# Attention followed by a feed-forward block on one core: outputs turned by the DMA, 288-token units, a smaller mask build

## The chip, the core and the metric

The kernel runs on one core of one Trainium2 chip. The metric is device time in microseconds of one launch. The program has five engines with queues of their own: TensorE (PE in the profile; PEld is its weight loading), VectorE (DVE), ScalarE (ACT), GpSimd (POOL) and SyncE (SP). POOL issues the loads and SP the stores; both sets of transfers run on the core's 16 DMA engines.

## What is computed

Eight batches of eight-head attention over 576 tokens with 64 features per head, and then a linear chain of matrix products over all 4608 tokens:

```python
batch, n_heads, seq, head_dim = (8, 8, 576, 64)
scores = scale * np.matmul(q, k.transpose(0, 1, 3, 2))
mask_plain = (rel >= 0) & (rel < 32)                                  # heads 0 to 3
mask_dil = (rel >= 0) & (rel < 32 * 4) & (rel % 4 == 0)               # heads 4 to 7
attn = softmax(np.where(masks, scores, -1e9))
x = np.matmul(attn, v).transpose(0, 2, 1, 3).reshape(B * S, H * D)    # 4608 x 512
a, b = x @ w1, x @ w2                                                 # 512 x 1024 each
out = (a * b @ w3) @ w_out                                            # 1024x1024, 1024x512
```

A query sees 32 keys. In a dilated head those keys lie four tokens apart, so a head splits into four residue classes of 144 tokens, each of them a plain sliding window.

## The kernel before, in words

All matrix data is bf16, sums are f32. The two last products are merged once: wf = w3 @ w_out (the W3 tasks, L494 to L516), so the feed-forward block is two products up (A with w1, B with w2), an elementwise product, and one product down with wf.

**Attention.** A batch has four steps: plain heads (u=0) and dilated heads (u=1), each in two halves of 288 tokens (hf), a half being three query blocks of 96. DVE turns q, k (and v of batches 0 and 1) to feature-major form with 32x32 transposes (`turn`, L276 and L289). Each step then is: scores on PE (`scores`, 24 small matmuls, L344), exponentials on ACT (`exps`, L354), mask product on DVE (`masks`, L360; batches 0 and 1 add a bias on PE before, L327, and skip it), values on PE (`values`, L377, two groups of six), reciprocal and normalization on DVE (L395, L401) into the tile `xo` (tokens by features), transposition back on PE (`back`, six matmuls with the identity, L412) into a PSUM bank, and a copy of that bank into the tile XT (features by tokens): `keep`, two copies of 288 columns per step, on ACT (L429) or DVE (L431). v of batches 2 to 7 comes straight from HBM into `vp` by many short runs (L196, L210).

**Feed-forward.** It works in tiles of 512 tokens (TB), nine of them. For each of eight feature blocks f it makes A (four matmuls of 512 columns, L442), copies it to SBUF on ACT (`copy_a`, L453, tile asb), makes B (four more), and multiplies both on DVE (`gate`, L457) into gt. Four `down` products per tile (eight matmuls of 512 columns, L464) give 128 output rows each; ACT copies them out (L475, osb) and SP stores them (L486). XT holds the tokens of all chunks in residue order (all tokens with remainder 0 by 4, then 1, 2, 3), so `store` scatters rows back with a step of four. Plain heads are brought into that order too: their queries are read with a strided pattern inside `scores`, and their mask has a pattern of its own for each half.

**Order.** All work is put into tasks, and `Plan.run` makes one static order for every engine from written-out durations, latencies and priorities (`add`). All PE results but the scores go through four PSUM banks ("places"): a task with slot=True takes a bank, which is free again when all tasks that read it are over. Scores have four banks of their own. Batches 2 and later are paced: a step's scores may start only after a certain A product (LEAD). POOL issues, in this order: q and k of batch 0 for u=0, the identity, q and k for u=1, v, the masks (`build_masks`, L241 to L263), w1/w2, w_out, w3, and then the loads of batch 1 and later.

Of the kernel before, what the change touches and what calls it, by code (L numbers as in the profile page):

```python
# [26 lines left out]
TB = 512  # L27
BIG = 30000.0
BIASED = 2
LEAD = 2.25  # L30
# [13 lines left out]
class Plan:  # L44
# [13 lines left out]
    def run(self):  # L58
# [22 lines left out]
        while len(order) < n:  # L81
            progress = True
            while progress:
                progress = False
                for e in engines:
# [25 lines left out]
                    for u in users[id(t)]:  # L111
                        left[id(u)] -= 1
                        if not left[id(u)]:
                            r = max(d.end + d.lat for d in u.deps)
                            waiting[u.eng].append((r, u))
# [12 lines left out]
def kernel(  # L128
# [19 lines left out]
    NT = n_tok // TB  # L148
# [16 lines left out]
    XT = const.tile([P, DCH, n_tok], BF16, name="XT")  # L165
    ident = const.tile([P, P], BF16, name="ident")
    mask = const.tile([P, 3, 3, QB], BF16, name="mask")
    vps = [const.tile([P, H, 6, PITCH], BF16, name=f"vp{i}") for i in range(2)]
    bias = const.tile([P, 3, 3, QB], BF16, name="bias")
# [4 lines left out]
    warm = const.tile([P, TB], BF16, name="warm")  # L174
# [65 lines left out]
    def build_masks():  # L240
        nc.gpsimd.memset(mask, 1.0)  # L241
        for i in range(3):
            m = mask[:, i, :, :]
            if i < 2:
                m, pat = m.rearrange("p m (r t) -> p m r t", r=4), [[0, 3], [1, 4], [4, 24]]
            else:
                pat = [[0, 3], [1, QB]]
            nc.gpsimd.affine_select(
                out=m, in_=m, compare_op=AL.is_ge, fill=0.0,
                base=32, pattern=pat, channel_multiplier=-1,  # L250
            )
            nc.gpsimd.affine_select(
                out=m, in_=m, compare_op=AL.is_ge, fill=0.0,
                base=-1, pattern=[[-a, n] for a, n in pat], channel_multiplier=1,
            )
            if i != 1:
                nc.gpsimd.memset(mask[0:32, i, 0, :], 0.0)
        late = mask[:, 2, 1, QB // 2 : QB]
        nc.gpsimd.affine_select(
            out=late, in_=late, compare_op=AL.is_ge, fill=0.0,  # L260
            base=-(32 + QB // 2), pattern=[[0, QB // 2]], channel_multiplier=1,
        )
        nc.gpsimd.tensor_scalar(  # L263
            out=bias, in0=mask, scalar1=-1.0, scalar2=BIG, op0=AL.add, op1=AL.mult
        )
# [47 lines left out]
    class Step:  # L313
# [4 lines left out]
        def kind(self):  # L318
            return 2 if self.u else self.hf

        def scores(self, biased=False):
            b, u, hf = self.b, self.u, self.hf
            qt, kt = qts[b % 2], kts[b % 2]
            self.sp = ps_s.tile([P, 4, TB], F32, tag="s", name="sp")
            if biased:
                for g in range(4):
                    nc.tensor.matmul(  # L327
                        out=self.sp[:, g, 0:VC],
                        lhsT=ident,
                        rhs=bias[:, self.kind(), :, :],  # L330
                        start=True,
                        stop=False,
                    )
            for mm in range(3):
                m = 3 * hf + mm
                for c in range(2):
                    for g in range(4):
                        prt = slice(32 * g, 32 * g + 32)
                        if u == 0:
                            qq = qt[prt, u, :, c].rearrange("p (r t) -> p r t", r=4)  # L340
                            qq = qq[:, :, 24 * m : 24 * m + 24]
                        else:
                            qq = qt[prt, u, QB * m : QB * m + QB, c]
# [12 lines left out]
        def masks(self):  # L356
            ev = self.et[:, 0 : 4 * VC].rearrange("p (g x) -> p g x", g=4)
            mk = mask[:, self.kind(), :, :].rearrange("p m x -> p (m x)")
# [48 lines left out]

        def back(self):
            self.x = bank([P, 2, 3, QB], BF16, "x")
            for pg in range(2):  # L410
                for mm in range(3):
                    nc.tensor.transpose(  # L412
                        out=self.x[:, pg, mm, :],
# [4 lines left out]
        def keep(self, pg, eng):  # L418
            c, t0 = 2 * self.u + pg, self.b * S
            if self.u == 0:  # L420
                dst = XT[:, c, t0 : t0 + S].rearrange("p (r t) -> p r t", r=4)
                for_m = dst[:, :, 72 * self.hf : 72 * self.hf + 72]
                dst = for_m.rearrange("p r (m t) -> p m r t", m=3)
                src = self.x[:, pg, :, :].rearrange("p m (r t) -> p m r t", r=4)
            else:
                dst = XT[:, c, t0 + VC * self.hf : t0 + VC * self.hf + VC]
                src = self.x[:, pg, :, :].rearrange("p m x -> p (m x)")
            if eng == "ACT":
                nc.scalar.copy(out=dst, in_=src)  # L429
            else:  # L430
                nc.vector.tensor_copy(out=dst, in_=src)  # L431
# [3 lines left out]
    gts, held = {}, {}  # L435

    def up(t, f, w_sb, key):
        if f == 0 and key == "a":
            gts[t] = wk_pool.tile([P, KFF, TB], BF16, tag="gt", bufs=3, name="gt")
        ps = bank([P, TB], F32, "ab")  # L440
        for c in range(DCH):
            nc.tensor.matmul(  # L442
                out=ps,
                lhsT=w_sb[:, c, f * P : (f + 1) * P],
                rhs=XT[:, c, t * TB : (t + 1) * TB],
                start=(c == 0),
                stop=(c == DCH - 1),
            )
        held[(key, t, f)] = ps

    def copy_a(t, f):
        a_sb = wk_pool.tile([P, TB], BF16, tag="asb", bufs=3, name="asb")
        nc.scalar.copy(out=a_sb, in_=held[("a", t, f)])  # L453
        held[("s", t, f)] = a_sb

    def gate(t, f):
        nc.vector.tensor_tensor(  # L457
            out=gts[t][:, f, :], in0=held[("b", t, f)], in1=held[("s", t, f)], op=AL.mult
        )

    def down(t, i):
        y = bank([P, d_model], F32, "y")
        for f in range(KFF):
            nc.tensor.matmul(  # L464
                out=y,
                lhsT=gts[t][:, f, i * P : (i + 1) * P],
# [4 lines left out]
        held[("y", t, i)] = y  # L471

    def copy_y(t, i):
        o_sb = wk_pool.tile([P, d_model], F32, tag="osb", bufs=3, name="osb")
        nc.scalar.copy(out=o_sb, in_=held[("y", t, i)])  # L475
        held[("o", t, i)] = o_sb

    def store(t, i):
        o_sb = held[("o", t, i)]
        c0, end = t * TB + i * P, t * TB + (i + 1) * P  # L480
# [41 lines left out]
    def warm_up():  # L522
        ps = bank([P, TB], F32, "warmps")
        for i in range(24):
            nc.tensor.matmul(out=ps, lhsT=warm[:, 0:P], rhs=warm, start=True, stop=True)

    def first_constants():
        nc.vector.memset(warm, 0.0)
        for t in kts + vts:
# [8 lines left out]
    add("warm", "PE", 7000, [c0], warm_up, 0)  # L538
# [36 lines left out]
    for u in range(2):  # L575
        loads_rows("qn", 0, (u,))
        loads_rows("kn", 0, (u,))
    loads_rows("vn", 0)
    idt = add("ident", "DMA", (600, 0), [], lambda: make_identity(nc, ident), 2.5, lat=-1900)
    mk = add("mask", "DMA", (3500, 0), [], build_masks, 5.5, lat=-1800)  # L580
# [7 lines left out]
    for ft in range(KFF):  # L588
        x = add("W3T", "PE", 450, [lw3[ft], idt], lambda f=ft: w3_back(f), 6, slot=True)
# [6 lines left out]
    kept, paced, pairs = {}, [], []  # L596
    prev = {"s": None, "e": [None] * 4, "x": [None] * 4}

    def turns(b, u, nm, pr):
        parts = (None,) if u == 0 and nm != "qn" else (0, 1)  # L600
# [9 lines left out]
    for b in range(B):  # L610
# [8 lines left out]
        T = {u: turns(b, u, "kn", 10 * b + 3) + turns(b, u, "qn", 10 * b + 3) for u in range(2)}  # L619
        if fast:  # L620
            vals = {}
            for u in range(2):
                tv = turns(b, u, "vn", 10 * b + 3)
                for half in range(2):
                    x = add(f"VT{b}.{u}", "PE", 330, tv + [idt],
                            lambda b=b, u=u, h=half: v_back(b, u, h), b - 99, slot=True)
                    last_v[(b, u)] = x
                    eng = "DVE" if u and half else "ACT"
                    vals[(u, half)] = [
                        add(f"VK{b}.{u}", eng, 1000, [x, c0],  # L630
                            lambda b=b, u=u, h=half, e=eng: v_keep(b, u, h, e), 10 * b + 1, lat=100)
# [5 lines left out]
        for i in range(4):  # L637
# [3 lines left out]
            if b < BIASED:  # L641
                s = add("S" + n, "PE", 980, T[u] + [mk, idt], lambda st=st: st.scores(True), b - 99,
                        after=[prev["s"]])
                m = e = add("E" + n, "ACT", 1150, [s], st.exps, 10 * b + 1, lat=100, after=[prev["e"][i]])
            else:
                s = add("S" + n, "PE", 480, T[u], st.scores, b - 99, after=[prev["s"]])
                e = add("E" + n, "ACT", 1150, [s], st.exps, 10 * b + 1, lat=100, after=[prev["e"][i]])
# [4 lines left out]
            for pg in range(2):  # L652
                vv = add(f"V{n}.{pg}", "PE", 190, [m] + vals[(u, hf)],
                         lambda st=st, pg=pg: st.values(pg), b - 99, slot=True)
                rc = add(f"R{n}.{pg}", "DVE", 160, [vv], lambda st=st, pg=pg: st.recip(pg), 10 * b + 1,
                         lat=0, after=[prev["x"][i], rc])
                ns.append(add(f"N{n}.{pg}", "DVE", 520, [vv, rc], lambda st=st, pg=pg: st.norm(pg),
                              10 * b + 1, lat=80))
            prev["e"][i] = vv
            x = add("X" + n, "PE", 270, ns + [idt], st.back, b - 99, slot=True)  # L660
            for pg in range(2):
                eng = "DVE" if pg and b >= 2 else "ACT"
                kept[b].append(
                    add(f"K{n}.{pg}", eng, 500 if eng == "ACT" else 320, [x],
                        lambda st=st, pg=pg, eng=eng: st.keep(pg, eng), 10 * b + 1, lat=100)
                )
            prev["x"][i] = x
# [4 lines left out]
    G, Y, gates, stores = {}, {}, [], []  # L672

    def ups(t, f):
        nonlocal seq
        need = [x for b in range((t * TB) // S, ((t + 1) * TB - 1) // S + 1) for x in kept[b]]
        seq += 1
        wl = lw12[f // 4]
        free = [Y[(t - 3, i)] for i in range(4)] if t >= 3 else []
        a = add(f"A{t}.{f}", "PE", 864, need + wl + free, lambda: up(t, f, w1_sb, "a"), seq, slot=True)  # L680
# [67 lines left out]
```

The softmax here doesn't subtract the row's maximum and nothing guards it: scores larger than these inputs give would overflow.

## Time and profile before

| | |
|---|---|
| median of 3 runs | 277.25 us (276.31 to 279.52) |
| time of the profiled execution | 276.21 us |
| its span (first to last instruction) | 274.5 us |
| mean granted TensorE clock | 0.994 |
| busy: PE, DVE, ACT, POOL | 258.3, 168.6, 124.7, 65.7 us |
| bytes moved by DMA | 29.22 MB, at a mean of 106 GB/s |
| first feed-forward matmul starts | 24.93 us |
| last step's attention output kept | 208.6 us |

Times in the profile count from the start of the span. In a row such as "L442 PE MATMUL ab<-XT,w_sb ... x576 | 135.7, 380 | 1.1" the numbers are the count, the busy time in us, the mean length of one in ns, and the time that the engine stood idle just before such instructions. Matmuls overlap in PE's pipeline: one of 512 columns shows as 380 ns, but eight of them follow each other in 1.73 us, 216 ns each; the chain of work shows that spacing.

### The profile page before, as it was taken

What the parts mean: (1) busy time and instruction counts of PE and PEld (TensorE: products, weight loads), DVE (VectorE), ACT (ScalarE), POOL (GpSimd) and SP (SyncE); (2) the same over time, 40 slices, a digit from 0 to 9 for tenths busy, and PEclk for the clock granted to TensorE, in tenths of its full rate; (3) what the DMA queues carried; (4) which work ended last, traced back from release to release, by engine and by line L of the source; (5) the groups of instructions that cost most, each with busy time, mean ns of one, the idle gap of its engine ahead of it and who ended that gap; (6) DMA issues with size and microseconds to landing.
All of it is one profiled execution on the core that took longest, in us unless ns stands there. A gap on an engine that the chain in (4) does not pass through costs nothing.

```text
span 274.5 us, 5945 instructions
## 1 busy us (share of the span) xinstructions
PE 258.3 (94%) x2440; PEld 132.8 (48%) x2440; DVE 168.6 (61%) x342; ACT 124.7 (45%) x207; POOL 65.7 (24%) x105
## 2 busy tenths in 40 slices
PE   8577997899889989999999999999999999999993
PEld 3264464466544554555455545555554444444441
DVE  3674435999999989999799555566654232242220
ACT  1166343568735636454455545544444423423421
POOL 8941451233692272017213300000000000000000
PEclk9989999999999999999999999999999999999999
DMA  6999999997999995819929602110111211201223
GB/s 103 182 205 207 210 211 211 188 96 119 173 136 119 189 126 70 196 41 200 134 49 94 100 15 62 42 41 38 41 41 38 70 44 41 76 38 38 78 76 118
DMA packets 43419, 29.22 MB, mean 106 GB/s; under 512 B 30080, under 2 KB 33152, under 8 KB 43392
## 3 DMA queue, kind: packets, MB, share of 16 engines
q0 software_dynamic: 37760, 19.40, 54.1%
q1 hardware_dynamic: 5632, 9.44, 11.0%
q8 instruction: 19, 0.31, 0.5%
q14 instruction: 8, 0.07, 0.1%
HBM read 38.80 MB, written 9.44 MB: 176 GB/s over the span
## 4 chain that ended last, share of the span: by engine, by line
PE 84%; DVE 7%; DMA 3%; issue 2%; ACT 1%; POOL 1%; DVEq 0%; ACTq 0%; POOLq 0%
PE ab L442 44%; PE y L464 22%; PE wf L506 5%; DMA vn<-in_v_dram 3%; PE sp L344 3%; PE vo L377 3%; DVE xo L401 3%; PE x L412 2%; PE vx L298 1%; PE x L494 1%; DVE rcp L395 1%; PE sp L327 1%; DVE et L360 1%; DVE gt L457 1%; DVE wf_sb L516 1%
## 5 line engine op out<-in xcount | busy, mean ns | idle before, releaser
L442 PE MATMUL ab<-XT,w_sb 128*128 128x512 bf16 x576 | 135.7, 380 | 1.1 <-ACT asb L453 0.7
L457 DVE TENSOR_TENSOR gt<-ab,asb 128x512 bf16<-128x512 f32 x72 | 49.3, 686 | 58.5 <-PE ab L442 53.5
L442 PEld LDWEIGHTS <-w_sb 128*128 128x128 bf16 x576 | 52.9, 98 | 58.7 <-issue 1.5
L464 PE MATMUL y<-wf_sb,gt 128*128 128x512 bf16 x288 | 67.4, 379 | 0.0
L453 ACT CAST asb<-ab 128x512 bf16<-128x512 f32 x72 | 42.1, 585 | 37.9 <-PE ab L442 35.0
L475 ACT COPY osb<-y 128x512 f32<-128x512 f32 x36 | 21.1, 586 | 73.9 <-PE y L464 73.9
L464 PEld LDWEIGHTS <-gt 128*128 128x128 bf16 x288 | 27.9, 98 | 33.1
L354 ACT ACTIVATE et<-sp 128x1152 bf16<-128x1152 f32 x32 | 36.6, 1143 | 16.0 <-PE sp L344 15.9
L210 POOL DMA_DIRECT2D vp<-in_v_dram x48 | 30.5, 644 | 32.0 <-PE vo L377 9.9
L401 DVE TENSOR_TENSOR xo<-vo,rcp 96x384 bf16<-96x384 f32 x64 | 35.2, 551 | 1.9
L289 DVE STREAM_TRANSPOSE qt<-qn 128x320 uint32<-128x320 uint32 (+1 forms) x32 | 21.6, 681 | 4.3 <-DMA qn<-in_q_dram 4.0
L377 PEld LDWEIGHTS <-et 128*128 128x128 bf16 x384 | 15.4, 98 | 7.3 <-DVE vp L311 0.9
L377 PE MATMUL vo<-vp,et 128*128 128x65 bf16 x384 | 17.7, 194 | 1.3 <-DVE vp L311 0.8
L360 DVE TENSOR_TENSOR et<-et,mask 128x1152 bf16<-128x1152 bf16 x24 | 17.8, 745 | 0.0
L429 ACT COPY XT<-x 128x288 bf16<-128x288 bf16 x40 | 15.1, 407 | 5.7 <-PE x L412 5.4
L412 PE MATMUL x<-ident,xo 96*128 96x96 bf16 x192 | 14.2, 207 | 2.2 <-DVE xo L401 2.1
L506 PE MATMUL wf<-wo_sb,w3T 128*128 128x512 bf16 x64 | 15.0, 380 | 1.2 <-ACT w3T L501 1.2
L395 DVE RECIPROCAL rcp<-vo 96x6 f32<-96x6 f32 x64 | 11.3, 180 | 6.6 <-PE vo L377 6.6
L412 PEld LDWEIGHTS <-xo 96*128 96x128 bf16 x192 | 11.0, 97 | 8.6 <-DVE xo L401 3.0
L344 PE MATMUL sp<-qt,kt 32*128 32x96 bf16 x768 | 14.3, 204 | 0.8 <-DVE qt L289 0.8
L344 PEld LDWEIGHTS <-kt 32*128 32x128 bf16 x768 | 9.7, 94 | 8.5 <-issue 6.4
L501 ACT COPY w3T<-x 128x1024 bf16<-128x1024 bf16 x8 | 8.1, 1013 | 10.9 <-PE wf L506 10.7
(44 smaller groups left out, 131.1 us busy)
## 6 DMA issues: line engine op xcount, KB each, us to landing
qn<-in_q_dram POOLq DMA_DIRECT2D x7, 576.0 KB, 7.5
kn<-in_k_dram POOLq DMA_DIRECT2D x7, 576.0 KB, 6.0
w_sb<-in_moe_w_dram POOLq DMA_DIRECT2D x4, 512.0 KB, 8.7
w3n<-in_moe_w_dram POOLq DMA_DIRECT2D x8, 256.0 KB, 14.9
out_dram<-osb SPq DMA_DIRECT2D x8, 256.0 KB, 2.3
out_dram<-osb SPq DMA_DIRECT2D x8, 224.0 KB, 2.4
vp<-in_v_dram POOLq DMA_DIRECT2D x6, 288.0 KB, 7.8
out_dram<-osb SPq DMA_DIRECT2D x8, 192.0 KB, 2.2
```

The source lines that it names most:

```text
L210: nc.gpsimd.dma_start(out=vp[32 + p0 : 32 + p0 + n, 4:8, m, 0:D], in_=v_rows(b, 4, 4 * t0 + res, [[4 * D, n], [S * D, 4], [1, D]]),)
L289: nc.vector.transpose(out=o, in_=i)
L344: nc.tensor.matmul(out=self.sp[:, g, QB * mm : QB * mm + QB], lhsT=kt[prt, u, QB * m : QB * m + P, c], rhs=qq, start=(c == 0 and not biase ...
L354: nc.scalar.activation(out=ev, in_=self.sp[:, :, 0:VC], func=ACT.Exp, scale=scale)
L377: nc.tensor.matmul(out=self.o[g // 2][:, g % 2, mm, :], lhsT=self.et[:, c0 : c0 + P], rhs=vp[:, 4 * self.u + g, 3 * self.hf + mm, 0 : D + ...
L401: nc.vector.tensor_tensor(out=self.xo[0:QB, :, gs, :].rearrange("p m g d -> p g m d"), in0=self.o[pg][0:QB, :, :, 0:D], in1=self.rcp[0:QB, ...
L412: nc.tensor.transpose(out=self.x[:, pg, mm, :], in_=self.xo[0:QB, mm, 2 * pg : 2 * pg + 2, :], identity=ident[0:QB, 0:QB],)
L442: nc.tensor.matmul(out=ps, lhsT=w_sb[:, c, f * P : (f + 1) * P], rhs=XT[:, c, t * TB : (t + 1) * TB], start=(c == 0), stop=(c == DCH - 1),)
L453: nc.scalar.copy(out=a_sb, in_=held[("a", t, f)])
L457: nc.vector.tensor_tensor(out=gts[t][:, f, :], in0=held[("b", t, f)], in1=held[("s", t, f)], op=AL.mult)
L464: nc.tensor.matmul(out=y, lhsT=gts[t][:, f, i * P : (i + 1) * P], rhs=wf_sb[:, f, :], start=(f == 0), stop=(f == KFF - 1),)
L506: nc.tensor.matmul(out=ps, lhsT=w3T[ft][:, g, :], rhs=wo_sb[:, g, :], start=(g == 0), stop=(g == KFF - 1),)
```

## The change

Five things are changed together.

1. The attention outputs of batches 2 to 7 are no longer turned on PE and copied. SP issues one DMA transpose per step, from `xo` to XT. Batches 0 and 1 keep the transposition on PE, with one ACT copy of 576 columns per step.
2. XT becomes two tiles (plain and dilated), in blocks of 96 tokens. Plain heads stay in token order: queries are read contiguously by block, and the feed-forward reads the plain chunks with a step of four elements.
3. The feed-forward goes in units of 288 tokens (16 units, half a batch each), with matmuls of 288 columns for A and B, a ring `gt` of 1152 tokens, and `down` products whenever 128 tokens are ready. A unit needs both plain halves and one dilated half of its batch. The chunks are summed in the order 2, 3, 0, 1.
4. The bias and mask have seven blocks of 96 columns instead of three patterns of 288. POOL makes one band (two selects of 96 columns and one of 48), DVE copies it into the blocks and makes the mask by a comparison.
5. The first loads come as q, k, v for u=0 and then for u=1. The warm-up on PE has 16 matmuls instead of 24, k and q of plain heads are turned in one instruction each, and durations and priorities of the plan are set anew. asb has four buffers instead of three.

```diff
+UNIT = 288
+RING = 1152
+TURNED = 2
+ORDER = (2, 3, 0, 1)
+WARM = 16
...
-    XT = const.tile([P, DCH, n_tok], BF16, name="XT")
+    XT = [const.tile([P, B * BLK, 2, QB], BF16, name=f"XT{u}") for u in range(2)]
+    gt = const.tile([P, KFF, RING], BF16, name="gt")
-    mask = const.tile([P, 3, 3, QB], BF16, name="mask")
+    mask = const.tile([P, 7, QB], BF16, name="mask")
...
+    def band():
+        base, mid = bias[:, 1, :], bias[:, 5, QB // 2 : QB]
         nc.gpsimd.affine_select(
+            out=base, in_=base, compare_op=AL.is_ge, fill=-BIG,
+            base=32, pattern=[[1, QB]], channel_multiplier=-1,
+        )
...
+    def blocks():
+        base = bias[:, 1, :]
+        nc.vector.tensor_copy(out=bias[:, 0:5:4, :], in_=base.unsqueeze(1).to_broadcast([P, 2, QB]))
+        nc.vector.memset(bias[0:32, 0:5:4, :], -BIG)
+        nc.vector.tensor_copy(out=bias[:, 2:4, :], in_=base.unsqueeze(1).to_broadcast([P, 2, QB]))
+        nc.vector.tensor_copy(out=bias[:, 5, 0 : QB // 2], in_=base[:, 0 : QB // 2])
+        nc.vector.tensor_copy(out=bias[:, 6, :], in_=base)
+    def masks_of_bias():
+        nc.vector.tensor_scalar(out=mask, in0=bias, scalar1=0.0, scalar2=None, op0=AL.is_ge)
...
-                        if u == 0:
-                            qq = qt[prt, u, :, c].rearrange("p (r t) -> p r t", r=4)
-                            qq = qq[:, :, 24 * m : 24 * m + 24]
-                        else:
-                            qq = qt[prt, u, QB * m : QB * m + QB, c]
+                        qq = qt[prt, u, QB * m : QB * m + QB, c]
...
+        def keep(self):
+            nc.scalar.copy(out=self.cols(), in_=self.x)
+        def back_dma(self):
+            nc.sync.dma_start_transpose(
+                out=self.cols().rearrange("p m g x -> p (m g) x"),
+                in_=self.xo[0:QB, :, :, :].rearrange("p m g d -> p (m g d)"),
+            )
...
+    def unit_cols(k, c):
+        b, hf = k // 2, k % 2
+        x = XT[c // 2][:, b * BLK : (b + 1) * BLK, c % 2, :]
+        if c < 2:
+            x = x.rearrange("p m (t r) -> p r m t", r=4)
+            return x[:, 2 * hf : 2 * hf + 2, :, :]
+        return x[:, 3 * hf : 3 * hf + 3, :]
+    def up(k, f, w_sb, key):
+        ps = bank([P, UNIT], F32, "ab")
+        for j, c in enumerate(ORDER):
             nc.tensor.matmul(
                 out=ps,
                 lhsT=w_sb[:, c, f * P : (f + 1) * P],
-                rhs=XT[:, c, t * TB : (t + 1) * TB],
+                rhs=unit_cols(k, c),
...
-    loads_rows("vn", 0)
+        for nm in ("qn", "kn", "vn"):
+            loads_rows(nm, 0, (u,))
...
-    parts = (None,) if u == 0 and nm != "qn" else (0, 1)
+    parts = (None,) if u == 0 else (0, 1)
...
+            if b < TURNED:
+                x = add("X" + n, "PE", 350, ns + [idt], st.back, b - 99 + RANK["X"], slot=True)
+                kept[b].append(add(f"K{n}", "ACT", 640, [x], st.keep, 10 * b + RANK["K"], lat=100))
+            else:
+                x = add("XD" + n, "SP", 100, ns, st.back_dma, 0, lat=3000)
+                kept[b].append(x)
...
+    for k in range(2 * B):
+        for f in range(KFF):
+            ups(k, f)
+            if f % 3 == 1 and done < n_y and (done + 1) * P <= k * UNIT:
+                downs(done)
+                done += 1
...
-        pair = int(9 * (b - LEAD) + 2.25 * i)
+        pair = int(16 * (b - LEAD) + 4 * i)
```

## The prediction

> **What bounds the kernel now.** I read the profile's busy times and slices first, then the busy times by stage, the waits of PE, the chain of work, and last the groups and timelines of the lines that the change touches.
>
> ```profile
> PE 258.3 (94%) x2440; PEld 132.8 (48%) x2440; DVE 168.6 (61%) x342; ACT 124.7 (45%) x207; POOL 65.7 (24%) x105
> GB/s 103 182 205 207 210 211 211 188 96 119 173 136 119 189 126 70 196 41 200 134 49 94 100 15 62 42 41 38 41 41 38 70 44 41 76 38 38 78 76 118
> ```
>
> PE is the bound of the whole, and the loads of the first 50 us run flat at 205 to 211 GB/s. By stage (each row: window, its length, then busy us and count of PE, PEld, DVE, ACT, POOL; granted clock, DMA share, GB/s):
>
> ```profile
> 10.00:25.00 15.00, 10.36 (x209) 7.50 (x209) 10.55 (x25) 8.80 (x19) 7.68 (x13) 0.89 1.18 197
> 80.00:100.00 20.00, 18.63 (x234) 9.72 (x231) 19.48 (x41) 9.76 (x15) 7.70 (x12) 1.00 1.31 159
> 120.00:140.00 20.00, 20.00 (x194) 9.99 (x193) 17.88 (x34) 10.26 (x17) 7.54 (x11) 1.00 0.97 142
> ```
>
> There are three stages. Until 25 us PE waits for a chain of loads, turns and masks. From 61 to 100 us DVE is full (17.97 of 19 us and 19.48 of 20) and PE not quite. From 100 us to the last product PE has no gap at all; its waits (engine, awaited engine, us in total, times, longest) from 61 to 262 us are only these:
>
> ```profile
> PE sp L344 <- DVE qt L289: 0.8, 1, 0.8
> PE ab L442 <- ACT asb L453: 0.7, 1, 0.7
> PE ab L442 <- DVE xo L401: 0.3, 1, 0.3
> PE vo L377 <- DVE XT L431: 0.3, 1, 0.3
> PE x L412 <- DVE xo L401: 0.2, 1, 0.2
> ```
>
> So from 100 us on every matmul removed is time, and every wait added is too. The chain of work from 115 to 125 us gives the true spacing of PE's work (start, length, what):
>
> ```profile
> 116.11 0.26 PE x L412 x6
> 117.24 0.36 PE vo L377 x12
> 119.33 0.86 PE ab L442 x4
> 120.45 0.37 PE sp L344 x22
> 122.65 1.73 PE y L464 x8
> ```
>
> A group of six x transposes holds PE for 0.26 us, although its busy time in the groups (207 ns each, pipelined) says more.
>
> **The change part by part.**
>
> *Transposes off PE.* 24 steps (batches 2 to 7) x 0.26 us = 6.2 us less on PE. With them go 24 ACT copies of 407 ns and 24 DVE copies of 302 ns, both beside PE.
>
> ```profile
> L429 ACT COPY XT<-x 128x288 bf16<-128x288 bf16 x40 | 15.1, 407 | 5.7 <-PE x L412 5.4
> L431 DVE COPY XT<-x 128x288 bf16<-128x288 bf16 x24 | 7.3, 302 | 9.0 <-PE x L412 7.5 <-ACT XT L429 1.1
> ```
>
> About 18 of the 24 lie after 100 us, where they are worth 4.7 us for sure. Six lie in the DVE-bound stretch; DVE loses six copies there, so I count all, -6.2, with -4.7 as the poor end.
>
> *What SP gets instead.* 24 DMA transposes of 96x768 go into SP's queue, in order between the stores; each waits for two normalizations, and stores queue behind it. A late normalization therefore delays a store, and the third osb buffer then holds up ACT's copy of y. Downs come at most every 5.2 us (3.6 pairs of 0.98 and one down of 1.73), so three buffers give some 10 us of slack. A store issue takes SP 366 ns (minimum, median, maximum below):
>
> ```profile
> L486 SPq DMA_DIRECT2D out_dram<-osb x64: 314/366/1537, 71.2 to 271.0; - x64
> DMA to landing us min/median/max: 1.6/2.3/7.0
> ```
>
> No transpose by DMA is in this trace. *Landing:* the nearest rows are the store (2.3 us) and the slowest load (w3n, median 14.9 us). In the instruction order of the changed program the values of step 2 of batch 2, which unit 4 needs, come some 22 us of PE work before it, and in later batches the distance is larger; at 14.9 us nothing waits, so landing costs 0 and the cover is the lead of attention over the feed-forward. A step's xo buffer is written again four steps later, which is far behind as well. *Issue:* per batch PE needs 16 pairs of A and B (15.7 us), 4.5 downs (7.8) and four steps (sp and vo, with the 0.1 us seam that follows sp in the chain, 0.84 each: 3.4), 26.9 us. Eight store issues take 2.9 us of SP, so SP keeps up while a transpose holds it for less than (26.9 - 2.9)/4 = 6.0 us. I take the store's 0.37 us, so 0 on the path; the upper end is the slowest load's 14.9, which would be far over. The store is the nearer row: same queue, similar size (147 KB here, 128 to 256 KB there).
>
> [...]
>
> *Units of 288.* Columns stay the same, 1024 x 288 = 576 x 512. Four bias matmuls of 288 columns take 0.49 us in the chain of work, 122.5 ns each; four of 512 take 0.864. So 1024 x 0.1225 - 576 x 0.2158 = 125.4 - 124.3 = +1.1 us. Weight loads (98 ns each, overlapping) hide behind 122 ns.
>
> *The strided reading of plain chunks* touches 512 of these matmuls (step of 8 bytes). Low end 0. For the high end the nearest row is sp: it reads at a step of 4 bytes, and 24 matmuls in 0.37 us, four side by side, are 61.7 ns per 96 columns, against 43 ns for a contiguous x matmul of 96 (0.26/6). Were that all the stride's doing, 1.43 x 122.5 would add 53 ns, 512 times, +27 us. But sp issues four matmuls and four weight loads in those 61.7 ns, which explains as much; I take 0.
>
> [...]
>
> *Evacuation.* Copy of A: between 585 ns (512 columns) and 1013 ns (1024) the slope is 0.836 ns per column, so 0.40 us for 288. Gate: from 551 ns (384) and 686 (512), 1.055 per column, 0.45 us. 128 of each: ACT 51 us instead of 42, DVE 58 instead of 49; ACT keeps slack, and DVE per batch (7.2 gates, 5.2 turns, 0.85 halo, 3.0 masks, 5.8 for eight reciprocals and normalizations) needs 22 of 26.9 us. What shrinks is tolerance: a bank must be free again within three tiles after its own, 3 x 0.49 = 1.5 us now, 2.6 before. An A behind an exponential is free after 1.14 + 0.40 + 0.2 = 1.74 us, 0.27 late, and there are 24 such steps; a B behind a whole plain turn (1.25 + 0.45 + 0.2) 0.4 late, 12 times. If all hit, 6.5 + 4.8 = +11.3 us. The low end is 0, since downs and steps between tiles add slack and the plan sets them there. The row that it is nearest to is PE's own wait for a copy, 0.7 us in one place. I take +2.
>
> *The start.* Before, the first scores wait for POOL's masks, and the values for all of v:
>
> ```profile
> 9.54 0.91 POOL L263 TENSOR_SCALAR bias<-mask 128x864 bf16<-128x864 bf16 x1
> 10.49 0.65 PE L327 MATMUL sp<-bias,ident 128*128 128x288 bf16 x4 [1.73 <-POOL bias L263]
> 13.26 1.26 DVE L276 STREAM_TRANSPOSE vt<-vn 128x576 uint32<-128x576 uint32 x1 [1.37 <-DMA vn<-in_v_dram]
> 24.93 2.41 PE L442 MATMUL ab<-XT,w_sb 128*128 128x512 bf16 x9
> ```
>
> Three POOL selects replace 5.6 us of mask work (4.87 to 10.45); at most 0.29 us each (the 128-column select), they are over near 4.5 us. q and k of u=1 are now issued behind v of u=0 and these selects, and land about one transfer later (288 KB at 205 GB/s, 1.4 us): q near 10.5, k near 12, v as before near 13.3, since bytes and rate are the same. Follow DVE, which the order of the changed program puts in series: turn q (5.5 to 6.8), five small copies (at most 0.3 each, the 288-column copy, but mostly smaller: 1.1), turn k (to 9.1), turn v (to 10.4), turn q of u=1 (to 11.9), mask (0.5), turn k (to 13.8), four DVE operations of step 0 (0.18 + 0.55, twice: 15.3), turn v (16.7), step 1 (18.2), v copies (19.3), step 2 (20.8), then transposes and the 0.64 us copy: first A near 22.2 instead of 24.9, since unit 0 needs three steps and not four. Change -2.7; ends 0 (the next batch's data, bound by 205 GB/s, comes no earlier and PE idles) and -4 (the DVE pieces overlap better). The weights are no obstacle: the first w_sb loads land near 18.7 us. I keep -2.7, because there is work for it: before, 16 of tile 0's 64 matmuls and every down are left for after the first scores of batch 1; now the order has one down and all wf products ahead of its second step.
>
> *The idle 61 to 100 us.* Counting that window by spacing (80 ab x 0.216, 32 y x 0.216, 120 vo, 60 x, 220 sp, 4 bias) gives about 35.2 us of work in 39, 3.8 idle. Smaller units can fill some; I take -1, ends 0 and -3.8.
>
> Warm-up (eight matmuls fewer) lies in PE's idle start, 0. The tail is the same: last down, copy 0.58, store.
>
> **Sum**: -6.2 + 1.1 + 0 + 2 - 2.7 - 1 = -6.8. The profiled execution took 276.21 us, 1.04 under the median of 277.25, so the sum gives 276.21 - 6.8 = 269.4 us.
>
> **The rivals.**
> 1. *The head start is swallowed.* Batch 1 arrives with the DMA, DVE stays the bound to 100 us, and the start's 2.7 and the six early transposes' 1.6 are lost: 273.7. For it speak the flat GB/s row and DVE at 19.48 of 20; against it the work left over in batch 0.
> 2. *Bank waits.* Half of the late frees hit, 5.7 instead of 2: 273.1; all of them, 278.7. For: DVE at 18 of 20 until 140 us, no gap in PE that could absorb a wait. Against: only one such wait before.
> 3. *More is filled*: the 3.8 idle us go and the frees cost nothing, start -4: 276.21 - 6.2 + 1.1 - 4 - 3.8 = 263.3.
> 4. *Slower: SP sets the pace.* A transpose holds SP's queue (or the transposes run one after another) for more than 6.0 us; each us over costs 24. It decides against the change when the sum's gain of 6.8 is used up, at 6.3 us; at 7 us the time is 293. For: nothing in the trace bounds it from above. Against: stores of that size take SP 0.37.
> 5. *Slower: the strided reading* costs more than 6.8/512 = 13 ns a matmul; at the sp row's 53 ns the time is 296.
>
> **How the numbers follow.** Forecast 0.42 (own range 266 to 272.5), rival 1 0.14, rival 2 0.14, rival 3 0.12, rival 4 0.12, rival 5 0.06. The measurement can tell about 1% (2.8 us) from no change. Faster by over 1% (under 274.5): 0.42 + 0.12, most of rival 1 (0.11) and of rival 2 (0.08), together 0.73; within 1%: the rest of rival 1 (0.03) and 0.04 of rival 2, 0.07; slower: rivals 4 and 5 and the end of rival 2 (0.02), 0.20. The range that leaves out rivals 4 and 5 and the rim of 3 is 262 to 278.
>
> **What would show it.** In the profile after: no x group for batches 2 to 7, so 48 x matmuls in all; ab spaced at 0.49 us per four; first ab near 22 us; PE without waits on asb or gt beyond 2 us in sum; SP's transpose issues under 1 us and landing under 15. PE busy in every slice after 100 us confirms the sum. The prediction is wrong if PE waits for XT behind a DMA, if SP's issues fill its time, if four ab matmuls take over 0.55 us, or if the slices between 25 and 100 us show more idle PE than before.

## The result, and the profile after

The changed kernel takes 333.08 us (median of 4 runs, 332.23 to 334.25) beside 276.82 us of the kernel before: a ratio of 1.200, with a 95% interval of 1.192 to 1.207. It is slower by a fifth; 269.4 was forecast, with a range up to 278. In two experiments below some runs were disturbed at a lower clock (two of six with the old order of loads, nine of twelve with batch 1 by DMA); their medians include those runs, their ratios do not, and the profiles shown of these two are of disturbed runs.

In the profile of the changed kernel, these lines stand where the lines of before stood (busy us, share of the span and count; then count, busy us, mean ns, and idle time before):

```profile
PE 318.3 (96%) x2706; PEld 177.4 (54%) x2736; DVE 173.0 (52%) x373; ACT 126.5 (38%) x231; POOL 61.5 (19%) x98
L454 PE MATMUL ab<-XT,w_sb 128*128 128x288 bf16 x1024 | 205.1, 360 | 1.2 <-ACT XT L430 0.7
```

PE is busier than before (318 us against 258) although it has work taken away, and its idle time before ab is 1.2 us in all. So next to nothing makes it wait; its own matmuls got longer. The stages say the same (window, length, busy us and count of PE, PEld, DVE, ACT, POOL, then granted clock, DMA share, GB/s):

```profile
61.00:100.00 39.00, 37.51 (x523) 22.32 (x525) 32.67 (x69) 22.32 (x38) 15.72 (x22) 1.00 1.12 135
100.00:140.00 40.00, 39.56 (x399) 22.10 (x403) 31.48 (x67) 16.25 (x28) 8.70 (x13) 1.00 0.92 131
```

DVE, busy 37.45 of the 39 us from 61 to 100 before, now has room there (32.67 of 39), at a granted clock of 1.00. The chain of work gives the spacing (start, us, what):

```profile
286.48 7.60 PE ab L454 x40
300.36 1.73 PE y L481 x8
302.09 7.60 PE ab L454 x40
```

Eight matmuls of y still take 1.73 us. But forty ab matmuls of 288 columns take 7.60, 190 ns each, where 122.5 was counted. Taken one by one from the trace, the four matmuls of a tile begin a median of 145, 122, 236 and 258 ns before the next one begins. With chunks summed in the order 2, 3, 0, 1, the last two are the plain chunks, which are read at a step of four elements. A tile costs 0.76 us instead of 0.49, and 256 tiles make 69 us. (A tile is one A or B product, four matmuls.) The prediction had named this sign: it is wrong "if four ab matmuls take over 0.55 us".

### The profile page after: what moved, and what is told of

Read it like the earlier page. It is cut to its first block, busy times and chain, and to the rows that moved or that the text cites. A ratio compares the mean times of both kernels' runs of the same rounds, so it can differ in the third digit from the quotient of the medians.

```text
span 331.5 us, 6739 instructions
## 1 busy us (share of the span) xinstructions
PE 318.3 (96%) x2706; PEld 177.4 (54%) x2736; DVE 173.0 (52%) x373; ACT 126.5 (38%) x231; POOL 61.5 (19%) x98
## 4 chain that ended last, share of the span: by engine, by line
PE 92%; DVE 2%; DMA 2%; ACT 2%; issue 1%; POOL 0%; POOLq 0%; ACTq 0%
PE ab L454 59%; PE y L481 18%; PE wf L523 4%; PE sp L351 3%; PE vo L384 3%; DMA vn<-in_v_dram 2%; DVE xo L408 1%; PE sp L338 1%; PE x L511 1%; PE vx L308 1%; ACT et L361 1%; PE x L423 1%; DVE vt L286 0%; ACT asb L465 0%; ACT osb L492 0%
## 5 line engine op out<-in xcount | busy, mean ns | idle before, releaser
L454 PE MATMUL ab<-XT,w_sb 128*128 128x288 bf16 x1024 | 205.1, 360 | 1.2 <-ACT XT L430 0.7
L454 PEld LDWEIGHTS <-w_sb 128*128 128x128 bf16 x1024 | 103.5, 104 | 73.6 <-issue 1.3
L470 DVE TENSOR_TENSOR gt<-ab,asb 128x288 bf16<-128x288 f32 x128 | 58.5, 457 | 123.6 <-PE ab L454 122.8
L465 ACT CAST asb<-ab 128x288 bf16<-128x288 f32 x128 | 51.0, 398 | 107.7 <-PE ab L454 107.2
L481 PE MATMUL y<-wf_sb,gt 128*128 128x512 bf16 x261 | 66.5, 382 | 1.3
L481 PEld LDWEIGHTS <-gt 128*128 128x128 bf16 x288 | 29.3, 102 | 35.3
L286 DVE STREAM_TRANSPOSE qt<-qn 128x576 uint32<-128x576 uint32 x8 | 10.0, 1246 | 2.9 <-DMA qn<-in_q_dram 2.9
L299 DVE STREAM_TRANSPOSE kt<-kn 128x320 uint32<-128x320 uint32 (+1 forms) x16 | 10.9, 681 | 0.7 <-PE sp L351 0.6
L299 DVE STREAM_TRANSPOSE qt<-qn 128x320 uint32<-128x320 uint32 (+1 forms) x16 | 10.9, 680 | 0.4 <-DMA qn<-in_q_dram 0.2
L195 POOL DMA_DIRECT2D kn<-in_k_dram x9 | 6.0, 671 | 23.7 <-DVE kt L299 22.7
```

The costliest lines, as they stand in the source:

```text
L299: nc.vector.transpose(out=o, in_=i)
L454: nc.tensor.matmul(out=ps, lhsT=w_sb[:, c, f * P : (f + 1) * P], rhs=unit_cols(k, c), start=(j == 0), stop=(j == DCH - 1),)
L465: nc.scalar.copy(out=a_sb, in_=held[("a", k, f)])
L470: nc.vector.tensor_tensor(out=gt[:, f, c0 : c0 + UNIT], in0=held[("b", k, f)], in1=held[("s", k, f)], op=AL.mult,)
L481: nc.tensor.matmul(out=y, lhsT=gt[:, f, c0 : c0 + P], rhs=wf_sb[:, f, :], start=(f == 0), stop=(f == KFF - 1),)
```

## The experiments

Theory: the step between neighbouring elements of the moving operand is the whole loss, and the other terms of the sum hold. The rivals were that small matmuls, the blocked layout with its short runs, or another engine's wait cost the time.

**e1_contig: the plain chunks read contiguously**

```diff
-            x = x.rearrange("p m (t r) -> p r m t", r=4)
-            return x[:, 2 * hf : 2 * hf + 2, :, :]
+            return x[:, 3 * hf : 3 * hf + 3, :]
```

> The changed kernel, but the two plain chunks are read as the dilated ones are: three contiguous blocks of 96 columns. This feeds the plain features of other tokens, so part of the computation is replaced; the work is the same in size. Theory (the strided reading is the whole loss): all four matmuls of an A or B tile follow each other at 122 ns instead of 122, 145, 236 and 258; 256 tiles lose 0.27 us each, 69 us, and the time falls from 333 to about 264. Rival 1 (the loss is in the smaller matmuls themselves, or in weight loads that no longer hide behind 288 columns): the spacing stays near 190 ns and the time near 333. Rival 2 (the stride costs, but DVE, ACT or SP are the next bound right behind it): the spacing is 122 ns inside a tile, but PE waits between tiles and the time ends between 275 and 300.

Measured: 265.85 us, ratio to before 0.962 (0.955 to 0.970); all four matmuls of a tile at 122 to 123 ns. The time falls by 67 us and the theory holds to 2 us. Both rivals fall: matmuls of 288 columns run at the rate of those of 512 (122 ns here, 216 there, 0.42 ns a column in both), and no other engine's wait takes the place of the loss.

**e2_residue: the same pattern with a step of one, correct data**

```diff
+                        if u == 0:
+                            qq = qt[prt, u, :, c].rearrange("p (r t) -> p r t", r=4)
+                            qq = qq[:, :, 24 * m : 24 * m + 24]
...
-            x = x.rearrange("p m (t r) -> p r m t", r=4)
+            x = x.rearrange("p m (r t) -> p r m t", r=4)
             return x[:, 2 * hf : 2 * hf + 2, :, :]
...
+        plain = bias[:, 0:4, :].rearrange("p m (r t) -> p m r t", r=4)
+        turned = base.rearrange("p (t r) -> p r t", r=4)
...
-        parts = (None,) if u == 0 else (0, 1)
+        parts = (None,) if u == 0 and nm != "qn" else (0, 1)
```

The last line lets DVE write the plain queries in residue order when it turns them, and the scores then read them from there.

> The changed kernel, but inside each block of 96 the plain heads' tokens stand in residue order (four runs of 24), as the queries are read in the kernel before, with the bias blocks permuted to match. A unit then reads the plain chunks as 2 x 6 runs of 24 elements with a step of one; the pattern has the same four dimensions as the strided one. Nothing is left out. Theory (the step between neighbouring elements costs, not the number of runs or dimensions): 122 ns per matmul, about 265 us. Rival (the many short runs, 24 elements each, cost): the plain matmuls stay above 150 ns and the time above 280.

Measured: 266.3 us, ratio 0.962 (0.957 to 0.968). The chain of work of this version:

```profile
206.82 4.90 PE ab L460 x40
211.72 1.73 PE y L487 x8
```

Forty matmuls take 4.90 us, 122.5 ns each, with twelve runs of 24 elements in every plain read. Runs and dimensions are free here (122.5 ns a matmul); the step is not (258). This version computes everything and is faster than both kernels. Repeated beside a later experiment (e12_residue_again, the same code):

> The residue-order version once more, beside the version with batch 1 by DMA and with more rounds. As before: 266.3 us, 0.962 of the kernel before, with an interval of about half a per cent either way.

Measured: 267.67 us, 0.965 (0.961 to 0.969).

**e3_step2, e10_step3, e7_step6, e4_step8, e9_step16: the size of the step**

Five runs of one execution each; the edits are shown in short form, one line to a run (two for step 3).

```diff
-            x = x.rearrange("p m (t r) -> p r m t", r=4)
-            return x[:, 2 * hf : 2 * hf + 2, :, :]
+            return x.rearrange("p m (t r) -> p r m t", r=2)[:, hf, :, :]          # step 2
+            return x.rearrange("p m (t r) -> p r m t", r=6)[:, 3*hf : 3*hf + 3]    # step 6
+            return x.rearrange("p m (t r) -> p r m t", r=8)[:, 4*hf : 4*hf + 4]    # step 8
+            return x.rearrange("p m (t r) -> p r m t", r=16)[:, 8*hf : 8*hf + 8]   # step 16
+            x = XT[0][:, b * BLK : (b + 1) * BLK, :, :].rearrange("p m g x -> p (m g x)")
+            return x.rearrange("p (t r) -> p r t", r=3)[:, 0, 0:UNIT]              # step 3
```

> The changed kernel with the plain chunks read at a step of two elements (4 bytes): 6 runs of 48. It feeds the plain features of other tokens, so part of the computation is replaced. Theory A (any step above one element halves the rate): the plain matmuls stay near 236 to 258 ns and the time near 333. Theory B (the price grows with the step in bytes; two elements in 4 bytes are half as dear as two in 8): plain matmuls near 122 to 180 ns, time 264 to 300. The scores read at this step too, 61.7 ns per four of 96 columns, which B with no price explains by the issue of four matmuls and A by the step.

> The changed kernel with the plain chunks read as one single run of 288 elements at a step of three (6 bytes), without inner dimensions. It feeds other features, so part of the computation is replaced. Theory A (62 ns per element of step, free up to two): 185 ns and a time near 300 us, the form of the pattern plays no part. Theory B (the count of dimensions and of run ends plays a part too): under 170 ns, time under 290. Theory C (a step that is no multiple of 4 bytes is dearer): over 240 ns, time over 325.

> The changed kernel with the plain chunks read at a step of six elements (12 bytes): 3 x 6 runs of 16. It feeds the plain features of other tokens, so part of the computation is replaced. Steps of 1, 2, 4 and 8 gave about 122, 129, 247 and 500 ns for a plain matmul. Theory A (time in proportion to the step above two elements, 62 ns per element of step): 370 to 380 ns, a time near 395 us. Theory B (the count of 16-byte lines that a run touches decides; at 12 bytes nearly each element lies in a line of its own, as at 16 bytes): 450 to 500 ns, a time near 440 to 460.

> The changed kernel with the plain chunks read at a step of eight elements (16 bytes): 4 x 6 runs of 12. It feeds the plain features of other tokens, so part of the computation is replaced. Theory A (a step costs the same whatever its size, half the rate): as the changed kernel, 333 us. Theory B (the price grows with the step, one line of 16 bytes for each element now): plain matmuls above 300 ns, the time above 365.

> The changed kernel with the plain chunks read at a step of sixteen elements (32 bytes): 8 x 6 runs of 6. It feeds the plain features of other tokens, so part of the computation is replaced. Steps of 4, 6 and 8 gave about 247, 374 and 500 ns. Theory A (proportional without end): about 990 ns, the time near 710 us. Theory B (a read fetches up to 16 bytes and each element now has its own; no further price beyond a step of 16 bytes): about 500 ns, the time near 460 to 500.

Measured, from the chain of work of each: a stretch of forty matmuls is ten tiles, one of 24 is six. In order: step 2, step 3, step 6, step 8, step 16, all at a granted clock of 0.99 to 1.00:

```profile
208.23 5.00 PE ab L453 x40
```

```profile
258.20 6.30 PE ab L454 x40
```

```profile
300.28 10.13 PE ab L454 x40
```

```profile
288.71 7.60 PE ab L454 x24
```

```profile
372.66 7.28 PE ab L454 x24
```

Two of a tile's four matmuls are strided, and the contiguous two take 0.245, so a strided one takes (tile - 0.245)/2:

| step, elements (bytes) | tile us | strided matmul, ns | whole run, us |
|---|---|---|---|
| 1 (2) | 0.490 | 122 | 265.9, 266.3 |
| 2 (4) | 0.500 | 128 | 269.8 |
| 3 (6) | 0.630 | 192 | 300.1 |
| 4 (8), the change | 0.760 | 258 | 333.1 |
| 6 (12) | 1.013 | 384 | 397.8 |
| 8 (16) | 1.267 | 511 | 500.3 |
| 16 (32) | 1.213 | 484 | 461.3 |

The price is linear, 64 ns per element of step, from two to eight, and rises no further at 16 elements (it is 5% lower there; why was not tried). Divide by the 16-byte pieces that 288 elements lie in (36, 72, 108, 144, 216, 288, 288): from step 2 on it is 1.7 to 1.8 ns for each piece, whatever the step, and at step 1 the 122 ns of the columns cover the 36 pieces. So a read that brings 16 bytes at a time fits all seven rows; that it is the unit is inferred from the end of the rise. For step 2 theory B was right, for step 3 theory A, for step 6 theory A, for step 8 theory B, for step 16 theory B. Theory B of step 6 had the unit that fits and a wrong count: at 12 bytes, 16 elements lie in 12 pieces, not in 16.

The run at step 8 was longer than its matmuls alone say, at a mean granted clock of 0.849; why the clock fell there was not tried. It shows one thing more. From 24 to 67 us its granted clock was 0.50 (start, us, what; then the row of that window):

```profile
24.68 35.47 PE ab L454 x96
24.00:67.00 43.00, 43.00 (x133) 17.38 (x132) 5.95 (x13) 8.24 (x17) 11.31 (x17) 0.50 0.95 150
```

A tile took 1.478 us there. Taken one by one from the trace, the second of the two contiguous matmuls took a median of 240 ns at this clock instead of 122, so a strided one took (1.478 - 0.480)/2 = 0.499 us, beside 0.511 at the full clock. In the run at step 16, at the clocks 0.50 and 1.00, the second strided matmul took 485 ns at both. As far as these two runs show, the price of the pieces does not follow the granted clock; that of the columns does.

**e8_before_step4: the step alone, in the kernel before**

```diff
-                rhs=XT[:, c, t * TB : (t + 1) * TB],
+                rhs=XT[:, c, t * TB : (t + 1) * TB].rearrange("p (t r) -> p r t", r=4)
+                if c < 2 else XT[:, c, t * TB : (t + 1) * TB],
```

> The kernel before, with its plain chunks read at a step of four elements inside each tile of 512 tokens, so the only suspected cost is added and nothing else of the change. The tokens of the plain features are permuted, so part of the computation is replaced. Theory (the step alone explains the loss): 288 of the 576 matmuls take about 427 ns instead of 216, twice as long, and the time rises by about 60 us to 337. Rival (the step costs only together with the small units or the blocked layout): under 290.

Measured: 343.73 us. The chain of work shows four tiles of 512 columns:

```profile
281.53 5.33 PE ab L442 x16
```

A tile takes 1.33 us instead of 0.86, a strided matmul 450 ns: 256 pieces of 16 bytes at 1.76 ns. The theory had 337 us. The step needs none of the rest of the change to cost what it costs.

**e5_residue_pe: what the DMA transposes are worth**

This edit and those of the two experiments after it are shown against the residue-order version (e2_residue).

```diff
-TURNED = 2
+TURNED = 8
```

> The residue-order version (266.3 us), with all 32 steps turned on PE and copied by ACT, so no DMA transpose is left (TURNED = 8). Nothing is left out of the computation. Theory (the sum's first term): PE gets 24 x 0.26 = 6.2 us of transposes back, ACT 24 copies of 0.64 us, and the time is 272.5. Rival 1 (the DMA transposes cost by themselves, by the transfers that they delay, the landing of 5 to 13 us and SP's queue): 266 or less. Rival 2 (more slots in the four banks and ACT copies of 0.64 us between the copies of A, on top of the 6.2): 275 or more.

Measured: 274.91 us, ratio 0.991 (0.987 to 0.994), so 0.026 to 0.028 of 277 us, 7 to 8 us, over the residue-order version, where 6.2 were counted. Where the 1 to 2 us over 6.2 come from was not pinned down, and rival 2 (275 or more) is not excluded: from 61 to 100 us PE is busy 35.60 of 39 us with the transposes on it and 36.61 without, but from 100 to 140 us 40.00 of 40 against 38.55.

**e6_oldloads: what the earlier start is worth**

```diff
-        for nm in ("qn", "kn", "vn"):
-            loads_rows(nm, 0, (u,))
+        loads_rows("qn", 0, (u,))
+        loads_rows("kn", 0, (u,))
+    loads_rows("vn", 0)
...
-    bnd = add("band", "DMA", (700, 0), [c0], band, 2.6, lat=-1800)
+    bnd = add("band", "DMA", (700, 0), [c0], band, 5.5, lat=-1800)
```

> The residue-order version (266.3 us) with the loads of batch 0 issued as before the change: q and k of u=0, then of u=1, then all of v, and the band on POOL behind them. Nothing is left out. Theory (the sum's start term): the first A product falls back from 21.4 us to between 23 and 25, and the time rises by as much, 2 to 3 us, to about 269. Rival (the head start is swallowed by the loads of batch 1 and by DVE up to 100 us): the first A product is as late, but the time stays within 1 us of 266.3.

Measured: 272.38 us, ratio 0.982 (0.977 to 0.987), 5 us over the residue-order version. The first A product of the residue-order version, then of this one:

```profile
21.40 0.65 PE L460 MATMUL ab<-XT,w_sb 128*128 128x288 bf16 x4 [0.73 <-ACT XT L436]
25.97 0.87 PE L460 MATMUL ab<-XT,w_sb 128*128 128x288 bf16 x4 [0.73 <-ACT XT L436]
```

PE waits 5.8 us for the bias, so this order starts even later than the kernel before (24.9), and both the start and the time moved more than the theory had (23 to 25, 269). The head start is not swallowed: the end moves by about as much as the start does (5 us and 4.6). How much of the 5 us is a lower clock was not separated: the granted clock of this profile is 0.50 to 0.56 from 10 to 20 us and 0.66 from 25 to 30, where the residue-order version has 1.00 in one profile, and in the other 0.70 from 20 to 25 us and 0.96 from 25 to 30.

**e11_turned1: batch 1 by DMA as well**

```diff
-TURNED = 2
+TURNED = 1
```

> The residue-order version with batch 1 turned by the DMA as well (TURNED = 1). Nothing is left out. Theory (each step moved off PE is worth its 0.26 us and an ACT copy, if the landing is covered): 1 to 1.5 us under the residue-order version. Rival (batch 1's outputs are needed as soon as they are there; normalization to landing takes 5 us and more, where the copy takes 1): the first A product of batch 1 waits for a transpose, and the time is 0 to 4 us over the residue-order version.

Measured: 279.41 us, ratio 0.995 (0.990 to 0.9995, from three executions), by the ratio 8 to 9 us over the residue-order version. The rival was right and its size too small. PE's waits (engine, awaited, us, times, longest):

```profile
PE ab L460 <- DMA XT<-xo: 6.9, 1, 6.9
```

From 61 to 80 us PE is busy only 10.63 of 19 us, and its granted clock is 0.84 there and 0.89 from 80 to 100 us, which may hold the rest of the loss. Here the cover is gone: batch 1's outputs are wanted as soon as they exist, and a transpose that lands 5.3 us (median) after its issue stands in the way.

## Why the prediction was wrong

**The step that failed is the strided reading.** The prediction put its low end at 0, its high end, from the sp row, at 53 ns a matmul or +27 us, and took 0. No run shows that 0; the runs showed +135 ns for each of 512 matmuls instead, +69 us, of which 67 show in the time. Two things were wrong in that step.

First, the bound was no bound. The sp row reads at a step of 4 bytes, the change at 8. The runs show that 4 bytes are nearly free (128 ns against 122 in a matmul of 288 columns). So the step explains little of sp's 61.7 ns per group, which said nothing of a step of 8; whether it is the issue of four matmuls was not tried. A row at a milder setting than the new one cannot bound it from above.

Second, no measurement stood behind the 0. Four matmuls and four weight loads in 61.7 ns were taken to explain sp's excess, but no row had the step without them, or them without the step; that was the author's estimate. The runs with the step alone decide: 128 ns at a step of two elements, 192 at three, 258 at four, beside 122 at a step of one, so that the step of the change reads at 0.47 of the rate (122/258). For TensorE's moving operand in bf16 a step of two elements was the largest measured that is nearly free.

Rival 5 named the cause and the point from which it decides (13 ns a matmul), but it was given a chance of only 0.06, and its price, 296 us, came from the false bound.

**The other terms, read from the residue-order version** (266.3 and 267.7 us, where the sum without the stride says 269.4):

*Transposes off PE:* -6.2 counted, -7 to -8 measured by e5. Right in kind, a little small.

*SP:* the forecast took 0.37 us of issue. The trace of the changed kernel has (minimum, median, maximum in ns, then in us):

```profile
L433 SPq DMA_TRANSPOSE XT<-xo x24: 1196/1200/2357, 83.9 to 248.8; - x24
DMA to landing us min/median/max: 2.3/3.7/8.6
```

SP is held 1.2 us, three times a store and over the 1 us that the prediction named as its sign, but far from the 6.0 at which it would set the pace. Landing takes 3.7 us for six 96x128 blocks, 5.3 (up to 12.6) in the quicker residue-order version, and nothing waits for it there: the 22 us of lead cover it. Rival 4 falls.

*Units of 288:* 122.5 ns per contiguous matmul as taken from the bias row; +1.1 stands.

*Bank waits:* +2 was taken. From 61 us to the last product, ab in the residue-order version waits for DVE as follows, the first at 123.7 us, when DVE itself had stood still for a load of q:

```profile
PE ab L460 <- DVE gt L476: 1.3, 1, 1.3
PE ab L460 <- DVE xo L414: 1.3, 2, 0.9
```

The second line is read as two more waits for a bank, since these products follow values whose banks a normalization frees. The repeat (e12) has the second line alone, and the kernel before had waits of this kind too, 1.0 us in all, so the term is 0.3 to 1.6. Rival 2, with 5.7, falls.

*The start:* first A forecast near 22.2 us. In the changed kernel:

```profile
7.69 0.65 PE L338 MATMUL sp<-bias,ident 128*128 128x288 bf16 x4 [1.35 <-DVE bias L270]
22.37 0.92 PE L454 MATMUL ab<-XT,w_sb 128*128 128x288 bf16 x4 [0.72 <-ACT XT L430]
```

Right here; in the residue-order version it is 21.4, 3.5 us earlier than before and not 2.7. That e6 moves the end with the start speaks against rival 1.

*The idle from 61 to 100 us:* -1 was taken. The items that the prediction lists there add up to 34.3 us, not "about 35.2", unless the 0.1 us seam after each sp is counted with them; the profile had PE idle 2.5 us. In the residue-order version:

```profile
61.00:100.00 39.00, 36.61 (x563) 24.52 (x563) 37.19 (x85) 22.43 (x37) 19.49 (x28) 1.00 1.34 156
100.00:140.00 40.00, 38.55 (x447) 25.72 (x445) 36.73 (x77) 18.40 (x34) 12.61 (x18) 1.00 1.37 178
```

PE is busy 36.61 of 39 us, against 36.48 before: no gain there, since DVE stays full (37.19 of 39); and the next stretch has 1.45 us of idle (0.47 in the repeat) where before had none. Rival 3, whose 263.3 lies as near to this version's time as the forecast does, wanted that idle time filled, and it was not.

So four of the sum's five signed terms were near. Without its failing term the sum was 2 to 3 us too high, and which terms hold these was not separated. The one term set at 0 outweighed all the rest ten times. The other parts of the change are a gain of 3.5 to 3.8%; the step of the reading alone turns it into a loss of 20%.

## What to carry to other kernels

Before a layout is changed to save a rearrangement, look at the innermost step with which TensorE then reads its moving operand: here two bf16 elements were nearly free (128 ns against 122), four doubled the matmul (258). Put the permutation where a strided write or read costs little: here it went into the queries' turn on DVE, before the scores, and a plain turn became two instructions, 682 ns each in the mean of all q turns, where the changed kernel has one of 1246 ns. Keep the runs contiguous: runs of 24 elements sufficed (122.5 ns a matmul). And when a price has no row of its own, ask of the bounding row whether it is at least as hard as the new case.

Here a transfer that takes work off the bounding engine was worth that work only where a lead covered its landing (5.3 us in the median): 7 to 8 us gained for batches 2 to 7, 8 to 9 us lost again by one more batch.

## What the runs showed of the hardware that was not expected

In these runs TensorE's moving operand in bf16 pays as if by the 16-byte pieces that it touches: 1.7 to 1.8 ns each, all but hidden behind the columns up to a step of two elements, and no more than one piece per element (511 ns at a step of 16 bytes, 484 at 32). In the run at step 8 the price stayed when the granted clock halved (499 ns at 0.50), while contiguous matmuls doubled from 122 to 240.

In the profile of the changed kernel this shows as a busy PE (96% of the span) at a granted clock of 1.00 from 61 to 140 us, with 1.2 us of idle before ab in all; only the spacing of equal matmuls, or the mean of the group (360 ns against 286 for the same 288 columns), gives it away.
